# Attention reads and scores in half-size matmul tiles, with the column sums moved behind the reads

## The chip, the cores and the metric

The kernel runs on one core of a Trainium2 chip. The metric is the device time of one execution in microseconds (us). TensorE (PE in the profile, its weight loads PEld), VectorE (DVE), ScalarE (ACT), GpSimd (POOL) and the DMA queues of SyncE (SP) and GpSimd work side by side, each on its own list of instructions in order, and wait for one another by semaphores.

## The reference

Two blocks follow one another. The first is an attention in both directions between the tokens of each of 8 batches and 8 heads (512 tokens, 64 features) and 32 state rows; the second is a feed-forward with a sine-square activation.

```python
scores  = scale * x @ state.T;   a  = softmax(scores);   xread = a  @ state    # 512 x 32 for each head
scores2 = scale * state @ x.T;   a2 = softmax(scores2);  sread = a2 @ x
y = concat([xread, sread])       # tokens first, then state rows; heads side by side: 4352 x 512 in all
h = y @ w_in                     # 512 -> 2048
g = h + sin(alpha * h)**2 / (alpha + 1e-9)
out = g @ w_out                  # 2048 -> 512
```

Nothing is subtracted from the scores before the exponential in the kernel, so scores and scores2 have the same exponentials E (one is the other transposed): xread needs row sums of E, sread column sums.

## The kernel before

All the work is written as small steps of a class, and a long hand-written list, ORDER, says in which order they are issued. A step is written with its arguments, as in `sc.4.0.5`: batch 4, group 0, PSUM bank 5. Each engine runs its own instructions in the order of that list; a step waits only where it needs data or a free bank. There are eight PSUM banks, and each step that starts a new result on TensorE names its bank; it waits until the last reader of the former content is done.

For a batch b, heads come in pairs (q = 0 to 3, two heads of 64 features fill the 128 partitions) and pairs come in groups of two (g). The steps are:

- `lx` loads x, `pk` packs it by token chunk (xp), `td` transposes it by DMA on SP's queue (xT). Batch 1 has `xt` and `xc` instead (transposes on TensorE, copies on ACT and DVE).
- `sc.b.g.bank` (line 399): the scores of group g, eight matmuls. The stationary tile is xT of a pair and a chunk of 128 tokens (128 rows, 128 columns); the moving operand is stT, the transposed state of the pair with zeros outside its two blocks, so 64 columns. `ex.b.g` (line 406) takes the exponential into E on ACT.
- `rs`, `rr` (DVE) are row sums and their reciprocals, `nm` (POOL) normalises E to A, `ad` transposes A by DMA on SP's queue into AT.
- `m.b.s.banks` (line 488) multiplies the state by w_in, in tiles of 64 rows and 32 columns, and `me` (line 496) copies that to M on ACT or DVE. `h.b.f` (line 537; `hg`, line 552, in batch 0) is then M times AT, 512 columns: 128 features of h for all tokens of the batch.
- `si`, `sq`, `gt` (lines 560, 569 or 201, 576) apply the activation; gt frees h's bank. `o.b.st.f0.f1` (line 587) sums over features into the output, `oc` copies it out of PSUM, `os` stores it from SP's queue.
- `w.b.bank` (line 450): the state reads. 16 matmuls: stationary, a pair of heads of xp for a chunk of tokens (128 rows, 128 columns); moving, E of that pair, 64 columns. Half of the result mixes two heads and is not used. `cs.b` (line 461) adds the column sums to the same bank, 8 matmuls with a stationary of ones of 64 columns, even and odd heads to the two halves of the partitions. `rc` and `xs` (DVE, lines 468 and 471) divide and put the result into xs_all, from which "batch" 8 (the state rows of all batches) takes its h (line 543).

In ORDER w and cs of a batch are neighbours in some batches and apart in others; cs.0, cs.2, cs.3 and cs.6 are issued directly ahead of an m block, and cs.7 and cs.5 directly after one another. The TensorE warm-up (`warm_up`) plays a part at the start only.

Of the kernel before, what the change touches and what calls it, by code (L numbers as in the profile page):

```python
# [9 lines left out]
ACT = mybir.ActivationFunctionType  # L10
ALU = mybir.AluOpType
AX = mybir.AxisListType
BF16 = mybir.dt.bfloat16
FP32 = mybir.dt.float32
# [27 lines left out]
o.0.2.5.6 xc.1.1.1.V xc.1.0.0.A o.0.0.6.7 xc.1.0.1.V o.0.0.7.8 o.0.2.6.7 sc.1.1.5 gt.0.10 sc.1.0.4  # L42
m.0.3.6.2 ex.1.0 o.0.2.7.8 me.0.3.0.V o.0.1.0.3.3 me.0.3.1.V o.0.1.3.6 hg.0.13.0.6 o.0.1.6.7 ex.1.1
rs.1.0 hg.0.13.1 m.1.3.2.4 si.0.13 o.0.1.7.8 rr.1.0 rs.1.1 nm.1.0.0.4.G o.0.1.8.9 hg.0.12.0.5
o.0.3.8.9 rr.1.1 hg.0.12.1 me.1.3.0.V o.0.0.8.9 nm.1.1.0.4.G o.0.1.9.10 o.0.0.9.10 me.1.3.1.V
si.0.12 o.0.0.10.11 o.0.3.9.11 sq.0.13.G ad.1 hg.0.15.0.2 sq.0.12.A o.0.1.10.12 hg.0.15.1 gt.0.12
o.0.2.8.10 si.0.15 o.0.2.10.11 gt.0.13 o.0.0.11.12 hg.0.14.0.4 sq.0.15.A hg.0.14.1 o.0.3.11.13
si.0.14 gt.0.15 o.0.0.12.13 o.0.1.12.13 o.0.3.13.14 sq.0.14.A pk.2.0.V o.0.1.13.14 pk.2.1.V h.1.2.5
gt.0.14 h.1.4.6 td.2 si.1.2 lx.3.0.1 h.1.0.2 si.1.4 o.0.0.13.15 sq.1.2.V h.1.1.4 si.1.0 gt.1.2
sq.1.4.G o.0.3.14.16 si.1.1 o.0.2.11.13 sq.1.0.A oc.0.3.V h.1.6.5 sq.1.1.G gt.1.4 o.0.2.13.14 os.0.3  # L50
h.1.3.0 si.1.6 gt.1.0 o.0.1.14.16 si.1.3 sq.1.6.G h.1.13.6 gt.1.1 oc.0.1.A o.0.2.14.15 o.0.0.15.16
si.1.13 h.1.15.2 sq.1.3.G gt.1.6 os.0.1 o.0.2.15.16 oc.0.0.A h.1.5.4 sq.1.13.G oc.0.2.V si.1.15
h.1.7.3 os.0.0 gt.1.3 o.1.1.0.1.5 si.1.5 os.0.2 h.1.8.1 sq.1.15.G gt.1.13 o.1.1.1.2 si.1.7
o.1.2.0.2.7 sq.1.5.A o.1.1.2.3 sq.1.7.G h.1.12.0 gt.1.15 si.1.8 h.1.9.6 gt.1.5 o.1.2.2.3 si.1.12
sq.1.8.G o.1.2.3.5 gt.1.7 si.1.9 o.1.1.3.4 h.1.10.2 sq.1.12.A pk.3.1.V h.1.11.4 sq.1.9.G gt.1.8
o.1.2.5.6 si.1.10 o.1.2.6.7 gt.1.12 h.1.14.3 si.1.11 sq.1.10.G o.1.2.7.8 gt.1.9 sc.2.1.1 si.1.14
o.1.1.4.7 sq.1.11.A pk.3.0.V sq.1.14.G o.1.1.7.8 gt.1.10 td.3 o.1.2.8.9 sc.2.0.0 o.1.1.8.9 gt.1.11
o.1.1.9.10 ex.2.0 o.1.3.0.2.6 gt.1.14 o.1.3.2.4 o.1.2.9.10 o.1.3.4.5 o.1.2.10.12 ex.2.1 o.1.2.12.13
rs.2.0 o.1.1.10.11 m.2.2.2.4.3.0 rr.2.0 rs.2.1 o.1.2.13.14 nm.2.0.0.4.G me.2.3.0.A o.1.2.14.15 w.0.1
rr.2.1 me.2.2.1.A me.2.3.1.V o.1.3.5.6 nm.2.1.0.4.G me.2.2.0.A o.1.3.6.7 o.1.2.15.16 cs.0 oc.1.2.A  # L60
m.2.0.3.4.0.2 ad.2 rc.0 o.1.3.7.8 me.2.1.1.A o.1.3.8.9 sc.3.0.7 xs.0.1 me.2.1.0.A o.1.1.11.12 os.1.2
me.2.0.0.V sc.3.1.2 me.2.0.1.A o.1.1.12.13 o.1.3.9.10 xs.0.0 o.1.3.10.11 ex.3.0 o.1.1.13.16 ex.3.1
rs.3.0 o.1.3.11.13 oc.1.1.A o.1.3.13.14 rr.3.0 h.2.0.0 rs.3.1 nm.3.0.0.4.G os.1.1 o.1.3.14.16 si.2.0
rr.3.1 h.2.1.3 oc.1.3.V nm.3.1.0.4.G h.2.2.4 h.2.8.1 os.1.3 h.2.3.7 lx.4.0.1 ad.3 si.2.2 o.1.0.0.3.2
si.2.8 sq.2.0.V o.1.0.3.4 sq.2.2.G gt.2.0 h.2.4.5 si.2.1 o.1.0.4.6 si.2.3 sq.2.8.G o.1.0.6.7 gt.2.2
h.2.9.6 si.2.4 o.2.3.0.1.0 o.1.0.7.8 sq.2.1.G o.1.0.8.9 sq.2.3.A gt.2.8 o.1.0.9.10 h.2.5.4 si.2.9
gt.2.3 o.1.0.10.11 sq.2.4.G o.1.0.11.12 si.2.5 h.2.7.1 gt.2.1 o.1.0.12.13 sq.2.9.A sq.2.5.G
o.1.0.13.14 gt.2.4 o.1.0.14.15 si.2.7 o.1.0.15.16 o.2.0.0.1.7 gt.2.9 o.2.0.1.2 oc.1.0.A h.2.6.3
sq.2.7.G gt.2.5 o.2.3.1.2 os.1.0 o.2.3.2.3 si.2.6 h.2.10.5 pk.4.1.V pk.4.0.V o.2.3.3.4 sq.2.6.A
o.2.3.4.5 gt.2.7 h.2.11.6 td.4 si.2.10 h.2.12.2 gt.2.6 si.2.11 o.2.0.2.3 sq.2.10.G o.2.0.3.4  # L70
o.2.3.5.6 si.2.12 h.2.15.4 h.2.13.1 sq.2.11.A gt.2.10 sq.2.12.G o.2.0.4.5 si.2.15 h.2.14.3 gt.2.11
o.2.3.6.7 si.2.13 o.2.0.5.6 sq.2.15.G gt.2.12 o.2.0.6.8 si.2.14 o.2.3.7.9 sq.2.13.A o.2.3.9.10
gt.2.15 sq.2.14.G o.2.0.8.11 gt.2.13 o.2.0.11.12 sc.4.0.5 sc.4.1.6 gt.2.14 o.2.3.10.12 ex.4.0
o.2.3.12.13 w.1.2 cs.1 o.2.0.12.13 rc.1 o.2.3.13.15 ex.4.1 o.2.3.15.16 m.3.0.4.1.3.5 rs.4.0 oc.2.3.A
o.2.0.13.14 me.3.1.0.A o.2.0.14.15 os.2.3 me.3.0.0.V o.2.1.0.1.6 me.3.0.1.A o.2.1.1.2 o.2.0.15.16
rr.4.0 rs.4.1 o.2.1.2.3 me.3.1.1.A nm.4.0.0.4.G h.3.1.0 oc.2.0.A o.2.1.3.4 rr.4.1 xs.1.0
m.3.2.3.4.1.5 si.3.1 nm.4.1.0.4.G os.2.0 xs.1.1 h.3.0.7 me.3.2.0.V h.3.2.2 ad.4 me.3.3.0.V o.2.1.4.6
lx.5.0.1 o.2.2.0.1.3 me.3.3.1.V si.3.2 o.2.2.1.3 si.3.0 h.3.6.1 sq.3.1.V sq.3.2.G me.3.2.1.V
h.3.14.5 si.3.6 o.2.2.3.4 gt.3.1 o.2.2.4.5 sq.3.0.G si.3.14 o.2.2.5.7 gt.3.2 o.2.2.7.8 sq.3.6.A
o.2.2.8.9 h.3.8.4 sq.3.14.G gt.3.0 h.3.5.0 si.3.8 gt.3.6 h.3.15.2 si.3.5 o.2.2.9.10 sq.3.8.G gt.3.14  # L80
o.2.2.10.11 h.3.9.7 si.3.15 h.3.7.1 si.3.9 sq.3.5.G gt.3.8 o.2.2.11.13 si.3.7 h.3.10.5 sq.3.9.G
o.2.2.13.14 sq.3.15.A gt.3.5 o.2.2.14.15 h.3.4.4 si.3.10 gt.3.15 o.2.1.6.7 sq.3.7.G o.2.1.7.8 si.3.4
o.2.2.15.16 o.2.1.8.10 sq.3.10.A gt.3.9 o.2.1.10.11 sq.3.4.G gt.3.7 o.2.1.11.13 oc.2.2.A o.2.1.13.14
gt.3.10 o.2.1.14.16 os.2.2 h.3.3.0 gt.3.4 oc.2.1.A h.3.12.2 si.3.3 pk.5.1.V o.3.2.0.1.7 os.2.1
m.4.2.1.3.5.6 pk.5.0.V si.3.12 sq.3.3.V td.5 o.3.3.0.1.4 me.4.2.1.V me.4.2.0.A o.3.2.1.2 sq.3.12.G
o.3.3.1.2 me.4.3.0.A o.3.2.2.3 gt.3.3 o.3.3.2.3 h.3.11.1 me.4.3.1.A gt.3.12 h.4.10.3 si.3.11 h.4.9.5
si.4.10 h.4.12.0 sq.3.11.V h.4.11.6 si.4.9 gt.3.11 sq.4.10.G o.3.2.3.5 si.4.12 o.3.2.5.7 sq.4.9.A
o.3.2.7.8 gt.4.10 sq.4.12.G o.3.2.8.10 si.4.11 o.3.2.10.11 gt.4.9 o.3.3.3.5 sq.4.11.A o.3.3.5.6
gt.4.12 o.3.3.6.8 m.4.0.2.1.3.5 gt.4.11 o.3.3.8.9 me.4.1.1.V me.4.0.1.A h.3.13.0 me.4.0.0.A h.4.8.6
me.4.1.0.V h.4.15.1 si.3.13 h.4.2.5 si.4.8 sq.3.13.V h.4.1.2 lx.6.0.1 si.4.2 gt.3.13 o.3.2.11.12  # L90
o.3.1.0.2.3 si.4.15 o.3.1.2.3 sq.4.8.V o.3.1.3.4 sq.4.2.G si.4.1 gt.4.8 o.3.3.9.12 sq.4.15.A h.4.3.0
sq.4.1.G gt.4.2 o.3.3.12.13 h.4.13.6 si.4.3 gt.4.15 o.3.3.13.15 si.4.13 sq.4.3.G o.3.3.15.16 gt.4.1
h.4.6.5 oc.3.3.A o.3.2.12.13 h.4.5.1 sq.4.13.G si.4.6 gt.4.3 os.3.3 h.4.14.2 si.4.5 o.3.0.0.1.4
sq.4.6.G o.3.2.13.14 gt.4.13 si.4.14 o.3.0.1.4 sq.4.5.A h.4.4.0 sq.4.14.G gt.4.6 o.3.0.4.5 h.4.0.6
si.4.4 gt.4.5 o.3.1.4.6 si.4.0 sq.4.4.G gt.4.14 o.3.2.14.16 w.2.5 sq.4.0.A pk.6.1.V o.3.1.6.7
oc.3.2.A h.4.7.1 pk.6.0.V gt.4.4 sc.5.0.2 td.6 si.4.7 o.3.1.7.8 sc.5.1.7 gt.4.0 o.3.1.8.9 o.3.0.5.6
ex.5.0 sq.4.7.G o.3.0.6.8 o.3.1.9.11 os.3.2 o.3.0.8.9 gt.4.7 o.3.0.9.12 cs.2 ex.5.1 rs.5.0
m.5.0.0.6.1.2 o.3.0.12.13 rr.5.0 me.5.0.0.A rs.5.1 o.4.3.0.1.7 nm.5.0.0.4.G o.3.0.13.14 me.5.0.1.A
o.3.0.14.15 rr.5.1 o.3.1.11.12 me.5.1.1.V o.3.1.12.13 me.5.1.0.A nm.5.1.0.4.G o.4.3.1.3 rc.2
o.3.0.15.16 o.4.3.3.4 o.3.1.13.14 oc.3.0.A ad.5 o.3.1.14.15 xs.2.0 m.6.0.0.6.2.1 xs.2.1 o.4.3.4.5  # L100
me.6.1.1.V me.6.1.0.A sc.6.1.4 os.3.0 sc.6.0.5 me.6.0.1.A o.4.3.5.6 me.6.0.0.V o.4.3.6.7 ex.6.0
o.4.3.7.8 o.4.0.0.1.2 o.3.1.15.16 ex.6.1 rs.6.0 w.3.1 oc.3.1.A cs.3 rr.6.0 m.5.2.6.0.5.4 rs.6.1
nm.6.0.0.4.G os.3.1 o.4.3.8.9 me.5.2.0.A me.5.2.1.V o.4.0.1.2 o.4.3.9.10 me.5.3.0.A o.4.3.10.11
rr.6.1 o.4.2.0.1.3 rc.3 nm.6.1.0.4.G o.4.2.1.2 me.5.3.1.A h.5.8.6 o.4.3.11.12 xs.3.1 h.5.9.0 si.5.8
ad.6 xs.3.0 o.4.0.2.3 o.4.3.12.14 o.4.2.2.4 h.5.4.5 si.5.9 o.4.3.14.15 sq.5.8.V h.5.3.4 si.5.4
gt.5.8 o.4.2.4.5 sq.5.9.G h.5.0.1 si.5.3 o.4.3.15.16 o.4.0.3.4 si.5.0 sq.5.4.G o.4.2.5.6 oc.4.3.V
o.4.2.6.8 sq.5.3.A gt.5.9 h.5.1.6 os.4.3 sq.5.0.G h.5.5.7 gt.5.4 si.5.1 o.4.2.8.10 si.5.5 gt.5.3
h.5.2.0 sq.5.1.G o.4.2.10.11 gt.5.0 o.4.2.11.12 si.5.2 h.5.14.5 lx.7.0.1 sq.5.5.A gt.5.1 h.6.3.4
o.4.2.12.13 si.5.14 gt.5.5 o.4.2.13.14 sq.5.2.G o.4.0.4.5 o.5.0.0.1.1 si.6.3 o.4.2.14.15 h.6.6.6
sq.5.14.A sq.6.3.G gt.5.2 o.4.0.5.6 h.5.13.7 si.6.6 gt.5.14 o.4.0.6.8 si.5.13 sq.6.6.G o.4.0.8.9  # L110
gt.6.3 o.4.0.9.11 sq.5.13.A o.4.0.11.12 h.6.2.0 gt.6.6 h.5.12.5 si.6.2 gt.5.13 o.4.2.15.16 h.6.4.4
si.5.12 sq.6.2.G o.4.0.12.13 oc.4.2.V o.4.0.13.14 si.6.4 o.4.0.14.15 o.4.1.0.1.6 os.4.2 o.4.1.1.2
# [551 lines left out]
```

The softmax here doesn't subtract the row's maximum and nothing guards it: scores larger than these inputs give would overflow.

## Time and profile before

| | |
|---|---|
| device time, median of 3 runs (lowest, highest) | 221.16 us (221.13, 221.43) |
| span of the profiled execution | 221.2 us; the view of the core gives 221.2 us too, and no other time lies around it |
| TensorE clock granted | 1.000 |
| score matmuls, line 399, 128\*128 with 64 columns | 128, median 193 ns each |
| state reads, line 450, 128\*128 with 64 columns | 128, median 193 ns each |
| column sums, line 461, 128\*64 with 128 columns | 64, median 219 ns each |
| weight loads of lines 399, 450, 461 | medians 98, 98, 110 ns |
| exponentials, line 406 | 16, median 597 ns |

A matmul's row lasts from its start to the end of its way through the array; matmuls overlap, so what one takes from the engine is read from the distance between starts. A shape such as 128\*64 is the stationary tile, rows by columns; "128x64 bf16" is the moving operand. An entry "idle ... <- X" says what ended the idle time before a row.

### The profile page before, as it was taken

What the parts mean: (1) busy time and instruction counts of PE and PEld (TensorE: products, weight loads), DVE (VectorE), ACT (ScalarE), POOL (GpSimd) and SP (SyncE); (2) the same over time, 40 slices, a digit from 0 to 9 for tenths busy, and PEclk for the clock granted to TensorE, in tenths of its full rate; (3) what the DMA queues carried; (4) which work ended last, traced back from release to release, by engine and by line L of the source; (5) the groups of instructions that cost most, each with busy time, mean ns of one, the idle gap of its engine ahead of it and who ended that gap; (6) DMA issues with size and microseconds to landing.
All of it is one profiled execution on the core that took longest, in us unless ns stands there. A gap on an engine that the chain in (4) does not pass through costs nothing.

```text
span 221.2 us, 4330 instructions
## 1 busy us (share of the span) xinstructions
PE 215.7 (97%) x1619; PEld 106.0 (48%) x1619; DVE 162.4 (73%) x286; ACT 173.5 (78%) x297; POOL 107.1 (48%) x115
## 2 busy tenths in 40 slices
PE   7999999999999999999999999999999999999994
PEld 3664454444444444444454444445445555665452
DVE  3468986999678979988888778889766988571201
ACT  3589878998899979998996999798857897685111
POOL 6866626595388728934863377363501072121000
PEclk9999999999999999999999999999999999999999
DMA  6999995953549518375325437380220211012042
GB/s 172 198 206 204 205 203 87 174 199 73 119 127 158 96 50 150 44 190 61 81 41 125 126 95 94 108 117 17 47 99 0 98 47 47 0 50 95 1 142 96
DMA packets 38052, 23.48 MB, mean 106 GB/s; under 512 B 20992, under 2 KB 33680, under 8 KB 38032
## 3 DMA queue, kind: packets, MB, share of 16 engines
q0 software_dynamic: 11648, 8.13, 26.1%
q1 hardware_dynamic: 26128, 15.08, 26.1%
q8 instruction: 12, 0.20, 0.4%
q14 instruction: 8, 0.07, 0.1%
q10 hardware_dynamic: 256, 0.01, 0.1%
HBM read 17.44 MB, written 8.91 MB: 119 GB/s over the span
## 4 chain that ended last, share of the span: by engine, by line
PE 93%; ACT 3%; DMA 2%; SPq 0%; issue 0%
PE o_ps L587 54%; PE h_ps L537 22%; PE m_ps L488 4%; PE h_ps L543 3%; PE h_ps L552 3%; DMA x<-in_x_dram 2%; PE s_ps L399 2%; PE warm_ps L303 2%; PE w_ps L450 2%; PE w_ps L461 1%; PE x_ps L361 1%; ACT L226 1%; ACT s L560 1%; ACT M L496 1%; PE x_ps L376 0%; PE st_ps L333 0%
## 5 line engine op out<-in xcount | busy, mean ns | idle before, releaser
L587 PE MATMUL o_ps<-w_out_sb,gT 128*128 128x512 bf16 (+2 forms) x560 | 137.7, 373 | 0.0
L576 DVE SCALAR_TENSOR_TENSOR gT<-s,inva_sb,h_ps 128x512 bf16<-128x512 bf16 (+1 forms) x144 | 96.6, 714 | 18.8 <-POOL s L201 9.6
L201 POOL TENSOR_TENSOR s<-s 128x512 bf16<-128x512 bf16 (+1 forms) x76 | 76.7, 1021 | 65.9 <-ACT s L560 62.4
L560 ACT ACTIVATE s<-h_ps,alpha_sb 128x512 bf16<-128x512 f32 (+1 forms) x144 | 88.8, 671 | 10.5 <-PE h_ps L543 4.3
L587 PEld LDWEIGHTS <-gT 128*128 128x128 bf16 x560 | 52.3, 98 | 60.3 <-issue 5.0
L537 PE MATMUL h_ps<-AT,M 128*128 128x512 bf16 x224 | 60.8, 379 | 0.0
L537 PEld LDWEIGHTS <-M 128*128 128x128 bf16 x224 | 21.7, 98 | 25.9 <-issue 0.4
L569 ACT ACTIVATE s<-s 128x512 bf16<-128x512 bf16 (+1 forms) x53 | 31.4, 595 | 0.8
L201 POOL TENSOR_TENSOR A<-E,rR 128x512 bf16<-128x512 bf16 x16 | 16.6, 1048 | 25.7 <-ACT o_sb L595 12.7
L595 ACT COPY o_sb<-o_ps 128x512 f32<-128x512 f32 (+2 forms) x24 | 13.7, 571 | 16.6 <-PE o_ps L587 16.5
L496 ACT CAST M<-m_ps 128x512 bf16<-128x512 f32 x35 | 18.6, 594 | 8.2 <-PE m_ps L488 8.1
L496 DVE CAST M<-m_ps 128x512 bf16<-128x512 f32 x29 | 18.9, 679 | 2.5 <-PE m_ps L488 2.1
L595 DVE COPY o_sb<-o_ps 128x512 f32<-128x512 f32 x11 | 7.6, 691 | 13.0 <-PE o_ps L587 12.9
L303 PE MATMUL warm_ps<-warm 128*128 128x128 bf16 (+3 forms) x66 | 9.9, 295 | 1.4 <-DVE warm L209 1.2
L410 DVE TENSOR_REDUCE R<-E 128x16 f32<-128x512 bf16 x16 | 10.4, 658 | 1.1 <-ACT E L406 0.9
L201 DVE TENSOR_TENSOR s<-s 128x512 bf16<-128x512 bf16 (+1 forms) x15 | 6.2, 415 | 6.8 <-ACT s L560 6.7
L488 PE MATMUL m_ps<-w_in_sb,stT 64*32 64x512 bf16 x256 | 10.2, 382 | 0.0
L468 DVE RECIPROCAL rC<-w_ps 128x128 f32<-128x128 f32 x8 | 7.6, 948 | 3.2 <-PE w_ps L461 3.2
L406 ACT ACTIVATE E<-s_ps 128x512 bf16<-128x512 f32 x16 | 8.8, 601 | 1.4 <-PE s_ps L399 1.3
L552 PE MATMUL h_ps<-AT,M 128*128 128x512 bf16 x32 | 9.4, 380 | 0.4 <-ACT M L496 0.4
L543 PE MATMUL h_ps<-xs_all,w_in_sb 128*128 128x256 bf16 x64 | 9.1, 273 | 0.0
L560 ACT ACT_TABLE_LOAD x5 | 6.4, 1283 | 2.2 <-PE h_ps L537 1.1
(56 smaller groups left out, 104.3 us busy)
## 6 DMA issues: line engine op xcount, KB each, us to landing
out_dram<-o_sb SPq DMA_DIRECT2D x33, 256.0 KB, 2.3
xnat<-in_x_dram POOLq DMA_DIRECT2D x7, 512.0 KB, 7.7
w_in_sb<-in_moe_w_in_dram POOLq DMA_DIRECT2D x4, 512.0 KB, 10.3
w_out_sb<-in_moe_w_out_dram POOLq DMA_DIRECT2D x4, 512.0 KB, 16.3
x<-in_x_dram SPq DMA_DIRECT2D x4, 256.0 KB, 4.3
st_nat<-in_state_dram POOLq DMA_DIRECT2D x1, 256.0 KB, 5.7
out_dram<-o_sb SPq DMA_DIRECT2D x1, 192.0 KB, 1.9
s<-in_state_dram SPq DMA_DIRECT2D x1, 128.0 KB, 2.1
```

What stands on the lines that cost most here:

```text
L201: {"V": k.nc.vector, "G": k.nc.gpsimd}[eng].tensor_tensor(out, a, b, ALU.mult)
L303: k.nc.tensor.matmul(wp[:, :cols], k.warm[:, 0:k.P], k.warm[:, :cols], start=True, stop=True)
L488: k.nc.tensor.matmul(k.t["m", b, s + n, g][o0:o0 + k.Ns, :], k.stT[k.half(r), b * k.G + g, c0:c0 + k.Ns], k.w_in_sb[k.half(r), 2 * g + h, ...
L496: k.copy(eng)(k.t["M", b][:, g, s * k.FW:(s + 1) * k.FW], k.t["m", b, s, g][:])
L537: k.nc.tensor.matmul(hp[:, :n], k.t["M", t][:, g, fs], k.t["AT", t][:, g, :], start=(g == 0), stop=(g == k.G - 1),)
L543: k.nc.tensor.matmul(hp[:, :n], k.w_in_sb[:, q, fs], k.xs_all[:, q].rearrange("p b j -> p (b j)"), start=(q == 0), stop=(q == k.Q - 1),)
L552: k.nc.tensor.matmul(k.t["h", t, f][:], k.t["M", t][:, g, f * k.P:(f + 1) * k.P], k.t["AT", t][:, g, :], start=(g == 0), stop=(g == k.G - 1),)
L560: k.nc.scalar.activation(s[:, :n], k.t["h", t, f][:, :n], ACT.Sin, scale=k.alpha_sb[:, f:f + 1])
L569: k.nc.scalar.activation(s2[:, :n], s[:, :n], ACT.Square)
L576: k.nc.vector.scalar_tensor_tensor(gT[:, :n], k.t["s2", t, f][:, :n], k.inva_sb[:, f:f + 1], k.t["h", t, f][:, :n], ALU.mult, ALU.add,)
L587: k.nc.tensor.matmul(k.t["o", t, st, half][:, cols], k.t["gT", t, f][:, rows], k.w_out_sb[:, f, cols], start=(f == 0), stop=(f == k.FT - 1),)
L595: k.copy(eng)(o_sb[:, cols], k.t["o", t, st, half][:, cols])
```

## The change

Two functions are rewritten or new, and the order is adapted.

- In `w` each matmul is split by head: a stationary of 64 columns (one head), 32 moving columns, to the head's own half of the partitions. 32 matmuls a batch instead of 16; the unused quarter blocks are no longer computed.
- `cs` stands directly behind `w` in every batch.
- For batches 1 to 7 `sc2` takes the place of the two `sc` steps. Each matmul takes one head: 64 rows of xT and of stT, 32 moving columns; even heads (r = 0) use rows 0 to 63 and write to one bank, odd heads (r = 1) rows 64 to 127 and another bank. 32 matmuls a batch instead of 16, in the order chunk, pair, head. `ex2.b.r` takes the exponential of the heads of one bank and puts them to their old places in E. Batch 0 keeps `sc` and `ex`. The bank numbers are the ones that the two `sc` steps had, in the order in which they stood; `sc2` stands where the second of them stood.

```diff
+    def sc2(k, b, *banks):
+        for r in range(2):
+            k.t["sc", b, r] = k.ps(banks[r], [k.P, k.G, k.C, 2, k.Ns], FP32, "s_ps")
+        for i in range(k.C):
+            for q in range(k.Q):
+                for r in range(2):
+                    g, h = q // 2, q % 2
+                    c = (2 * h + r) * k.Ns
+                    k.nc.tensor.matmul(
+                        k.t["sc", b, r][:, g, i, h, :], k.t["xT", b][k.half(r), i, q, :],
+                        k.stT[k.half(r), b * k.G + g, c:c + k.Ns], start=True, stop=True,
+                    )
+    def ex2(k, b, r):
+        E = k.new(b, "E", k.epool, [k.P, k.G, k.C, k.P], BF16)
+        k.nc.scalar.activation(
+            E[:].rearrange("p g c (h r j) -> p (g c h) r j", r=2, j=k.Ns)[:, :, r, :],
+            k.t["sc", b, r][:].rearrange("p g c h j -> p (g c h) j"), ACT.Exp, scale=k.scale,
+        )
...
     def w(k, b, bank):
...
         for q in range(k.Q):
             for i in range(k.C):
-                k.nc.tensor.matmul(
-                    wc[:, q, 0:2 * k.Ns], k.pair(b, i, q),
-                    E[:, q // 2, i, (q % 2) * 2 * k.Ns:(q % 2 + 1) * 2 * k.Ns],
-                    start=(i == 0), stop=(i == k.C - 1),
-                )
+                for r in range(2):
+                    c = (q % 2 * 2 + r) * k.Ns
+                    k.nc.tensor.matmul(
+                        wc[k.half(r), q, r * k.Ns:(r + 1) * k.Ns],
+                        xp[:, i, 2 * q + r, :], E[:, q // 2, i, c:c + k.Ns],
+                        start=(i == 0), stop=(i == k.C - 1),
+                    )
```

In ORDER, with the neighbours on TensorE (the rest of the list is as it was; ex becomes ex2 in place):

```diff
-o.0.2.6.7 sc.1.1.5 gt.0.10 sc.1.0.4 m.0.3.6.2
+o.0.2.6.7 gt.0.10 sc2.1.5.4 m.0.3.6.2
-sc.2.1.1 ... o.1.2.8.9 sc.2.0.0 o.1.1.8.9
+o.1.2.8.9 sc2.2.1.0 o.1.1.8.9
-w.0.1 ... o.1.2.15.16 cs.0 oc.1.2.A m.2.0.3.4.0.2 ... o.1.3.8.9 sc.3.0.7 ... o.1.1.11.12 ... sc.3.1.2 ... o.1.1.12.13
+w.0.1 cs.0 ... o.1.2.15.16 oc.1.2.A m.2.0.3.4.0.2 ... o.1.3.8.9 ... o.1.1.11.12 ... sc2.3.7.2 ... o.1.1.12.13
-o.2.0.11.12 sc.4.0.5 sc.4.1.6 gt.2.14 o.2.3.10.12
+o.2.0.11.12 sc2.4.5.6 gt.2.14 o.2.3.10.12
-w.2.5 ... sc.5.0.2 ... o.3.1.7.8 sc.5.1.7 ... o.3.1.8.9 ... cs.2 ex.5.1 rs.5.0 m.5.0.0.6.1.2
+w.2.5 cs.2 ... o.3.1.7.8 sc2.5.2.7 ... o.3.1.8.9 ... ex2.5.1 rs.5.0 m.5.0.0.6.1.2
-sc.6.1.4 os.3.0 sc.6.0.5 ... w.3.1 oc.3.1.A cs.3 rr.6.0 m.5.2.6.0.5.4
+os.3.0 sc2.6.4.5 ... w.3.1 cs.3 oc.3.1.A rr.6.0 m.5.2.6.0.5.4
-w.4.2 ... o.5.2.4.5 sc.7.1.5 gt.6.1 sc.7.0.0 o.5.2.5.7 ... h.6.13.6 rs.7.0 cs.4
+w.4.2 cs.4 ... o.5.2.4.5 gt.6.1 sc2.7.5.0 o.5.2.5.7 ... h.6.13.6 rs.7.0
-w.5.1 ... o.5.3.13.14 ... w.7.4 gt.7.7 si.7.0 cs.7 os.5.3 cs.5 h.7.5.3
+w.5.1 cs.5 ... o.5.3.13.14 ... w.7.4 cs.7 gt.7.7 si.7.0 os.5.3 h.7.5.3
```

w.1 with cs.1, and w.6 with cs.6, stood together already.

## The prediction

> **What bounds the kernel now.** I read the page's head first, then its chain, then TensorE's rows by shape, and last the timelines around the steps that change.
>
> ```profile
> span 221.2 us, 4330 instructions
> ...
> PE 215.7 (97%) x1619; PEld 106.0 (48%) x1619; DVE 162.4 (73%) x286; ACT 173.5 (78%) x297; POOL 107.1 (48%) x115
> ...
> PEclk9999999999999999999999999999999999999999
> ...
> PE 93%; ACT 3%; DMA 2%; SPq 0%; issue 0%
> ```
>
> TensorE is busy for 97% of the span and carries 93% of the chain. From 28 to 205 us the busy time by windows is 177.00 of 177.00 us, at a granted clock of 1.00. So from there on a nanosecond added to TensorE's stream is a nanosecond of span, and one taken out is won, as long as nobody else becomes late. The profiled span, 221.2 us, is as good as the median of the three runs (221.16), so I add the sum to 221.2 without a correction. A measurement of this kernel can tell about 0.2%, 0.44 us, from no change: under 220.7 is faster, over 221.6 slower.
>
> TensorE's timeline around the reads of batch 0 (start, length, line, shape, count) gives all prices:
>
> ```profile
> 55.82 0.60 PE L587 MATMUL o_ps<-w_out_sb,gT 128*128 128x512 bf16 x2
> 56.26 0.63 PE L450 MATMUL w_ps<-E,xp 128*128 128x64 bf16 x16
> 56.72 0.81 PE L587 MATMUL o_ps<-w_out_sb,gT 128*128 128x512 bf16 x3
> 57.47 0.41 PE L461 MATMUL w_ps<-E,ones 128*64 128x128 bf16 x8
> 57.81 0.63 PE L488 MATMUL m_ps<-w_in_sb,stT 64*32 64x512 bf16 x16
> 58.37 0.39 PE L587 MATMUL o_ps<-w_out_sb,gT 128*128 128x512 bf16 x1
> ```
>
> Lengths overlap, so I subtract starts.
> - *Same shape.* 56.72 - 56.26 = 0.46 us for 16 state reads is 29 ns each; the two o matmuls before took 216 and 216 (+10 once, below). The single rows give 55.5 ns at 128 columns, 109 at 256, 162.5 at 384, 216 at 512: columns / 2.4 plus 2.4 ns, with the next load hidden.
> - *A change of tile shape.* Three o matmuls should take 0.65 us, but 57.47 - 56.72 is 0.75. In the single rows each of the 46 changes after 12 us between 128\*128, 128\*64 and 64\*32 adds 92 to 108 ns, mostly 93 to 96: I take 94. The first load in the new shape is exposed on top: 10 ns for 128\*128 or 64\*32, 24 for 128\*64 (first matmuls of 390, 387 and 243 ns against 379, 376 and 219). So 104 ns, or 118 into 128\*64.
> - *Column halves run side by side.* The eight column-sum matmuls start in pairs 4 ns apart, a pair each 55 ns; both of the first pair are late by the same 24 ns, so the two loads ran together.
>
> **Reads and column sums (w, cs).** Each batch's 16 reads of 128\*128 with 64 columns become 32 of 128\*64 with 32 columns: 16 pairs. A pair's stream is 32 / 2.4 + 2.4 = 15.7 ns, but its loads need 24, and steady rows start a load 1 to 2 ns after the previous matmul: I take 27 ns. The row of today's pair (29) and a load just hidden (26) are near; an unhidden load is 24 + 15.7 = 40, loads one after the other 54. Gain: 8 x 16 x (29 - 27) = 0.26 us. What it costs is the shape. Today w needs no change of shape and cs has both. With cs behind w the pair shares them, but cs loses its old neighbours: cs.0 and cs.2 stood ahead of an m block (57.47 to 57.81 above), so one exit served as m's entry: one more change each. cs.7 and cs.5 ran as one block of 16:
>
> ```profile
> 171.56 0.63 PE L450 MATMUL w_ps<-E,xp 128*128 128x64 bf16 x16
> 172.12 0.64 PE L461 MATMUL w_ps<-E,ones 128*64 128x128 bf16 x16
> 172.69 0.60 PE L537 MATMUL h_ps<-AT,M 128*128 128x512 bf16 x2
> ```
>
> They are split: two more. Batches 1, 3, 4 and 6 stay equal (there w is only drawn into the shape). Four changes, one of them into 128\*64: 118 + 3 x 104 = 0.43 us. Net **+0.17 us** (from -0.2 at 24 ns a pair to +1.8 at 40). cs needs only E, long ready; rc and xs keep their order on DVE, and rc may start earlier, which costs nothing.
>
> **Scores (sc2).** Batches 1 to 7 change 16 matmuls of 128\*128 with 64 columns (464 ns) into 32 of 64\*128 with 32, even heads on rows 0 to 63, odd heads on 64 to 127, one bank each. No row of before has the shape 64\*128; the m block (64\*32), where row halves start 3 to 4 ns apart, is nearest. A pair's step lies between 15.7 ns (the stream, by the line through all columns seen) and 29 (the row of 64 columns, the shortest step that the trace has). I take 22, the middle, and keep both ends. Loads of 128 columns were exposed by 10 ns only, so a step of 15.7 would hide them.
>
> Each sc2 stands between 128\*128 matmuls, so it enters and leaves: 2 x 104 = 208 ns, against 16 x (29 - 22) = 112 saved: +96 ns for each of batches 2 to 7, **+0.58 us** (0.0 at 15.7 ns, +1.25 at 29). The trace cannot show that 64\*128 is a change. The Trainium skill (TensorEngine Tiling (Array Packing), Tiling Modes, Key Properties) says that changing the mode, not just the tile, drains TensorE, and lists 64x128 as a mode of its own; that would make it 208 ns, against 0 if only column tiles cost.
>
> The same page (Performance Considerations, Instruction Overhead) speaks against the change: about 60 cycles for each matmul, so that one with a single column takes as long as one with 60, and no tiling factor should be taken from a dimension that is already small. Today's 64 columns at 29 ns agree; an estimate by that page, 60 / 2.4 = 25 ns a pair, would make the scores dearer by 7 x 16 x 3 = 0.34 us than my 22.
>
> Batch 1 is different, because its xT is made by copies just ahead:
>
> ```profile
> 28.97 0.91 DVE L385 COPY xT<-x_ps 128x512 bf16<-128x512 bf16 x2 [0.62 <-ACT xT L385]
> ...
> 29.50 0.73 PE L399 MATMUL s_ps<-stT,xT 128*128 128x64 bf16 x16
> 30.16 0.41 PE L488 MATMUL m_ps<-w_in_sb,stT 64*32 64x512 bf16 x8
> ```
>
> The second copy (heads 2 and 3) ends at 29.88 and releases TensorE at 29.94. Today heads 4 to 7 go first (sc.1.1), then 0 and 1, and only the last four matmuls wait, 94 ns. sc2 goes through all heads for each chunk, so its third matmul already needs that copy: TensorE stands from 29.5 to 29.94, with the entry inside that wait. Then 16 x 22 = 0.35 and the change to m, 0.09: 0.88 us in place of 0.66, **+0.22 us** (+0.12 to +0.33). Batch 3 likewise: sc.3.1 had 0.17 us between the copy that frees its bank (me.2.1.1.A) and its start, and the 0.23 us of sc.3.0 ahead of it go: **+0.06 us**. The other sc2 blocks have 0.1 us or more; sc.4 starts 0.1 us after its transposed xT lands (issue at 72.55 plus the median 4.3 us), all of it in one DMA as before. No DMA is moved: steps of TensorE alone change place.
>
> **The new wait.** ex2.b.0 fills only even heads, so rs.b.0 needs both exps. On ACT they stand back to back:
>
> ```profile
> 53.62 1.09 ACT L406 ACTIVATE E<-s_ps 128x512 bf16<-128x512 f32 x2
> ...
> 54.25 0.69 DVE L410 TENSOR_REDUCE R<-E 128x16 f32<-128x512 bf16 x1
> ```
>
> So rs.2.0 moves from 54.25 to about 54.73, 0.48 us. In batches 3, 5, 6 and 7 it is 0.45 to 0.5 too; rs.1.0 and rs.4.0 start after the second exp already. Behind it on DVE queue rr, rs.b.1 and a copy of M or o_sb; behind those POOL's nm and SP's transpose ad, with the output stores behind it. The cover: A^T of batch 2 lands at 57.45 + 3.0 = 60.45 and h.2 starts at 61.44; for batch 5 123.0 and 125.48, the others have 7 us and more, save batch 1, whose rs does not move. DVE itself waits 1.25 us after batch 2's block and 0.94 after batch 3's. I price it at **0.1 us** (0 to 0.5: the wait uncovered once). The exps keep their size; their write goes in runs of 32, and ACT's 591 to 628 ns stay within the same cover.
>
> **Sum:** 0.17 + 0.58 + 0.22 + 0.06 + 0.1 = +1.13 us, so 221.2 + 1.1 = **222.3 us**.
>
> **Rivals.**
> - *Faster (10%): a change to 64\*128 is free.* Place: the two ends of each sc2. With 15.7 ns a pair batches 2 to 7 win 6 x 16 x 13.3 = 1.28 us; batch 1 still loses 0.12, batch 3 0.06, w 0.17: 220.3 us. It decides below about 40 ns a change (12 changes, 1.28 - 0.35 - 0.44 left). For it: no row of that shape. Against it: all shapes that the trace has pay 92 or more, and 64\*32 has row halves too.
> - *No change (13%): changes cost, halves stream.* At 15.7 ns a pair batches 2 to 7 come out even, batch 1 +0.12, w between -0.2 and +0.17: 221.2 to 221.6.
> - *Much slower (13%): halves do not overlap.* Reads at 40 ns a pair: 8 x 16 x 13 = 1.7 more, 224.0; at 54 it is 225.8. Scores one after the other, 31 ns a pair: +1.1, 223.4. Against it: the column-sum pairs and the m block run side by side.
> - *My forecast (64%)*, 221.7 to 223.5: the upper end has 29 ns a score pair (+0.78) and 30 ns a read pair (+0.38).
>
> The range is 221.0 to 224.5: it begins where the second rival does, less the spread of the runs, and leaves out the free change and the worst of the third rival. Faster 0.10, same 0.13, slower 0.77.
>
> **What would show it.** Right: from an o row to the first 64\*128 row about 0.31 us, and the same out again; 64\*128 and 128\*64 pairs at 15 to 29 ns; TensorE's wait at 29.5 to 29.94; rs.2.0 right behind the second exp; TensorE without other gaps. Wrong: o rows 216 ns ahead of sc2 (the free change), pairs of 40 ns or more, or an h matmul of batch 2 or 3 that waits for A^T or M.

## The result and the profile after

| | before | after |
|---|---|---|
| device time, median (lowest, highest) | 221.21 us (221.13, 221.43; 6 runs) | 224.09 us (223.12, 225.86; 6 runs) |
| ratio after / before, 95% interval | | 1.0125 (1.0091 to 1.0160) |
| span of the profile shown | 221.2 us | 224.0 us |
| TensorE clock granted | 1.000 | 1.000 |

The change costs 2.9 us. The forecast was 222.3 us, 1.1 us more than before, in a range of 221.0 to 224.5: the sign and the range hold, the size does not, and the narrower 221.7 to 223.5, which had 64% of the chances, does not hold the median either. In the runs from here on the device time lies about 1.9 us above the span; a span of 221.2 us would be 223.1 us, which no run of before has. So the profile of before that the prediction used (span 221.2 us) is of an execution that began slowly: against a second profile of before (span 219.2 us, 221.06 us) it loses 2 us between 6 and 10 us, and all its later rows stand 1.9 to 2.1 us later. Up to 10.3 us its matmuls of 128 columns start 107 ns apart, those of the second profile 55 ns from 5.3 us on; the granted clock reads 1.000 in both. I compare with the second one.

The page of after, its head, chain and DMA queues:

```profile
span 224.0 us, 4804 instructions
...
PE 215.4 (96%) x1859; PEld 103.5 (46%) x1859; DVE 162.7 (73%) x286; ACT 173.6 (78%) x297; POOL 107.0 (48%) x115
...
PEclk9999999999999999999999999999999999999999
...
q8 instruction: 14, 0.23, 0.4%
...
PE 82%; DMA 8%; ACT 4%; DVE 2%; POOL 2%; issue 1%; SPq 0%; POOLq 0%; ACTq 0%
```

Two things differ from the page of before. TensorE's part of the chain fell from 93% to 82% and DMA's rose from 2% to 8%. That alone proves no new wait, as the second profile of before has 86% and 6%; the waits are read below. And the program has 474 instructions more (4804 against 4330). The program is itself read over the DMA engines, in packets of 16 KB of queue q8, one for about 120 pairs of weight load and matmul on TensorE: 14 packets instead of 12. TensorE's own new work is read from its timeline (start, length, line, shape, count), at the reads of batch 0 and the scores of batch 3:

```profile
55.98 0.60 PE L609 MATMUL o_ps<-w_out_sb,gT 128*128 128x512 bf16 x2
56.51 0.68 PE L472 MATMUL w_ps<-E,xp 128*64 128x32 bf16 x32
57.04 0.39 PE L483 MATMUL w_ps<-E,ones 128*64 128x128 bf16 x8
57.37 0.82 PE L609 MATMUL o_ps<-w_out_sb,gT 128*128 128x512 bf16 x3
58.12 0.62 PE L510 MATMUL m_ps<-w_in_sb,stT 64*32 64x512 bf16 x16
58.67 0.82 PE L609 MATMUL o_ps<-w_out_sb,gT 128*128 128x512 bf16 x3
59.43 0.57 PE L412 MATMUL s_ps<-stT,xT 64*128 64x32 bf16 x32
59.93 2.12 PE L609 MATMUL o_ps<-w_out_sb,gT 128*128 128x512 bf16 x9
```

By starts: three o matmuls of 216 ns and the entry into 64\*128 take 59.43 - 58.67 = 0.76 us, so the entry is about 0.10; the single rows give 96 ns, and 13 for the first loads, by which the second pair starts late. The 32 half-height score matmuls and the way out take 59.93 - 59.43 = 0.50 us; the single rows give 89 ns and 11 for the load on the way out, and 25.2 ns a pair (21 and 4). The 32 reads take 57.04 - 56.51 = 0.53 us, where the 16 of before took 0.46: 31.6 ns a pair (28 and 3), and 21 for the first loads.

What TensorE waits for between 33 and 79 us, in the view of the waits (us in total, times, longest), first in after, then in the second profile of before:

```profile
PE h_ps L559 <- DMA AT<-A: 1.5, 1, 1.5
PE h_ps L559 <- DVE gT L598: 0.9, 1, 0.9
```

```profile
PE o_ps L587 <- issue: 0.2, 1, 0.2
```

TensorE's timeline of after shows the first of them; the second profile of before, shown behind it, has the same 6 o matmuls followed by h at once:

```profile
35.97 1.46 PE L609 MATMUL o_ps<-w_out_sb,gT 128*128 128x512 bf16 x6
38.97 0.81 PE L559 MATMUL h_ps<-AT,M 128*128 128x512 bf16 x3 [1.54 <-DMA AT<-A]
```

```profile
35.60 1.46 PE L587 MATMUL o_ps<-w_out_sb,gT 128*128 128x512 bf16 x6
36.89 0.81 PE L537 MATMUL h_ps<-AT,M 128*128 128x512 bf16 x3
```

Step by step against the second profile of before, after ends 4.84 us later: 0.12 from the start, 1.9 of TensorE's own work, 1.71 for the transposed A of batch 1, 1.05 ahead of h.2.13 for gt.2.7, and 0.1 ahead of the scores of batch 4. "Own work" means here and below what TensorE's changed steps take longer, without waits. This profile is the slowest run of after; the median is 1.8 us shorter, and the fastest of the six, 223.12 us, is before plus the 1.9 us of own work.

### The profile page after: what moved, and what is told of

Read it like the earlier page. It is cut to its first block, busy times and chain, and to the rows that moved or that the text cites. A ratio compares the mean times of both kernels' runs of the same rounds, so it can differ in the third digit from the quotient of the medians.

```text
span 224.0 us, 4804 instructions
## 1 busy us (share of the span) xinstructions
PE 215.4 (96%) x1859; PEld 103.5 (46%) x1859; DVE 162.7 (73%) x286; ACT 173.6 (78%) x297; POOL 107.0 (48%) x115
## 4 chain that ended last, share of the span: by engine, by line
PE 82%; DMA 8%; ACT 4%; DVE 2%; POOL 2%; issue 1%; SPq 0%; POOLq 0%; ACTq 0%
PE o_ps L609 47%; PE h_ps L559 19%; DMA xnat<-in_x_dram 4%; PE m_ps L510 3%; PE h_ps L565 3%; DMA AT<-A 2%; PE w_ps L472 2%; PE h_ps L574 2%; DMA x<-in_x_dram 2%; POOL A L200 2%; PE s_ps L412 2%; PE warm_ps L302 1%; ACT s L582 1%; PE w_ps L483 1%; DVE xp L347 1%
## 5 line engine op out<-in xcount | busy, mean ns | idle before, releaser
L302 PE MATMUL warm_ps<-warm 128*128 128x128 bf16 (+3 forms) x66 | 8.6, 271 | 1.4 <-DVE warm L208 1.2
L419 ACT ACTIVATE E<-s_ps 128x512 bf16<-128x512 f32 x14 | 7.7, 603 | 0.4 <-PE s_ps L412 0.4
```

The costliest lines, as they stand in the source:

```text
L302: k.nc.tensor.matmul(wp[:, :cols], k.warm[:, 0:k.P], k.warm[:, :cols], start=True, stop=True)
```

## The experiments

The kernels are before or after with small edits. The expectations of the first four do not have the instruction fetch yet. In them one reading is that TensorE's own work and two waits, both caused by the new order, make up the whole; the other is that the wait for batch 1 is due to the faster start of the profiled execution. The later ones set "theory F" (the waits come from where a 16 KB instruction fetch falls) against these. Each time is compared with runs of before that were taken with it: medians 221.31 us for experiments 1 to 4 and 221.51 for 5 to 8. Experiments 1, 9 and 10 are single runs; 9 and 10 have one run of before beside them, 220.83 us.

**1. Before once more**, unchanged, for a profile with a normal start.

> The kernel before, unchanged, for a second profile. Theory A (the sum): the whole difference of 2.9 us is made after the 28th microsecond, by TensorE's own time (17 shape changes at 104 to 118 ns, read pairs at 31.6 ns, score pairs at 25.2 ns, as the profile after has them) and one late chain (1.06 us); the start is noise that a wait of TensorE for the transposed A of batch 1 swallows, so this profile may start up to 1.9 us sooner than the first one and still end within 0.3 us of it. Theory B (the start): the first profile happened to have a slow start of 1.9 us, and with a fast one TensorE has no wait for that transpose; then the span here is about 219.3 us, and the wait of 1.7 us at h.1.2 in the profile after belongs to the change.

Measured: 221.06 us, span 219.2. It starts about as early as after does, and does not wait for the transposed A of batch 1. So an early start alone does not make the wait.

**2. The reads alone**: the new `w` with `cs` behind it; scores as before.

```diff
+                for r in range(2):
+                        wc[k.half(r), q, r * k.Ns:(r + 1) * k.Ns],
+                        xp[:, i, 2 * q + r, :], E[:, q // 2, i, c:c + k.Ns],
...
-w.2.5 ... cs.2 ex.5.1
+w.2.5 cs.2 ... ex.5.1
```

> Only the reads in half-width matmuls with the column sums behind; scores as before. Theory A: four more shape changes, 0.43 us, and 8 x 16 pairs at 31.6 ns where 29 stood, 0.33 us: about 222.0 us (+0.76), and no new wait. Theory C (waits are all): TensorE's extra time is swallowed by waits elsewhere, 221.2 us.

Measured: 223.71 us, ratio 1.0121 (1.0104 to 1.0139), span 221.8. TensorE's own steps are 0.76 us longer: 8 x 16 x (31.6 - 29) = 0.33 for the pairs and 0.43 for four shape changes. Of the span's 2.65 us over experiment 1 another 0.45 stands at the start, and the rest, 1.45 by the starts, is one wait ahead of the scores of batch 4, in a place that the edit does not touch. Neither reading had it (222.0 and 221.2 us):

```profile
73.14 2.54 PE L589 MATMUL o_ps<-w_out_sb,gT 128*128 128x512 bf16 x11
76.99 0.64 PE L399 MATMUL s_ps<-stT,xT 128*128 128x64 bf16 x16 [1.31 <-DMA xT<-xp]
```

Of the transpose td.4 that it waits for, 15 of 16 landings come between 75.23 and 75.38 us, the 16th at 76.94. A 16 KB packet of the instruction queue began at 74.92 us and took 938 ns, to 75.86; the last packet of the transpose ends at 75.88. The trace does not name a packet's DMA engine; that the late landing is of the engine which carried the instructions is inferred from this. In the second profile of before that fetch comes at 76.5 us, after td.4 has landed (74.77 to 74.90).

**3. The scores alone**: `sc2` and `ex2` for batches 1 to 7; reads and column sums as before.

```diff
-sc.2.1.1 ... sc.2.0.0
+sc2.2.1.0
```

> Only the scores head by head; reads and column sums as before. Theory A: 13 shape changes at 104 ns, 1.35 us, less 7 x 16 x (29 - 25) ns, 0.45 us, plus some 0.3 us of wait in batch 1, plus the late chain through POOL (row sums after both exps, then the normalisation, then the load of batch 4's x, then its packing on DVE, then gt.2.7, then h.2.13), 1.06 us: about 223.4 us (+2.2). Theory C: without the late chain 222.4 us.

Measured: 223.34 us, ratio 1.0096 (1.0079 to 1.0113), span 221.9. Own work about +1.2 us, and a wait of 1.42 us for the transposed A of batch 1. There is no wait of more than 0.1 us ahead of h.2.13, for which I had put 1.06: the number expected (223.4) came out for another reason. Here the third instruction fetch comes at 34.1 us, in the middle of the transposes that SP issues from 33.27 us on; in before at 39.3 us.

**4. After with the load of x for batch 4 ahead of `nm.3.0`** on POOL, to take away the wait ahead of h.2.13, which came through this load.

```diff
-rs.3.1 nm.3.0.0.4.G ... h.2.3.7 lx.4.0.1 ad.3
+rs.3.1 lx.4.0.1 nm.3.0.0.4.G ... h.2.3.7 ad.3
```

> The changed kernel with the load of batch 4's x (lx.4.0.1) issued on POOL ahead of batch 3's normalisation (nm.3.0) in place of behind it. Theory A: the load starts at least 2 us sooner, DVE's packing no longer waits for it, gt.2.7 is on time, and TensorE's wait of 1.06 us ahead of h.2.13 goes: 223.0 us in place of 224.1. Rival: another wait stands behind it (the slow packing copy of 1.28 us beside POOL's work) and at most 0.3 us come back: 223.8 us.

Measured: 228.91 us, ratio 1.0344 (1.0314 to 1.0373): far off both numbers. POOL issued the load at 56.85 us, and it ran beside the transposes ad.2. The DMA issues from 57 to 66 us (queue, KB, median us to landing), here and then in after:

```profile
xnat<-in_x_dram POOLq DMA_DIRECT2D x1, 512.0 KB, 9.1
out_dram<-o_sb SPq DMA_DIRECT2D x2, 256.0 KB, 7.3
AT<-A SPq DMA_TRANSPOSE x1, 8.2
```

```profile
out_dram<-o_sb SPq DMA_DIRECT2D x3, 256.0 KB, 2.9
xnat<-in_x_dram POOLq DMA_DIRECT2D x1, 512.0 KB, 8.2
AT<-A SPq DMA_TRANSPOSE x2, 3.0
```

The transpose took 8.2 us in place of 3.0, and h.2.0 waited for it. The place of the load behind `nm` had kept the two apart; nothing is won there.

**5. Before with 32 more instructions at the start**: eight early warm-up groups of two matmuls of 128 columns become four of 32. All else is before, unchanged.

```diff
-warm_up.2.128.3 ex.0.0 warm_up.2.128.4 lx.1.0.1
+warm_up.4.32.3 ex.0.0 warm_up.4.32.4 lx.1.0.1
```

> The kernel before, with eight of the early warm-up groups (two matmuls of 128 columns) cut into four matmuls of 32: 16 more matmuls and 16 more weight loads on TensorE ahead of the first scores, nothing else. Theory F (instruction fetch): the 16 KB fetches of the program are tied to the number of instructions issued, so those after the early stage come some 0.5 to 5 us sooner; if one falls into the transposes of ad.1 (33 to 37 us) or td.4 (74 to 77 us), h.1 or sc.4 waits 1.4 to 1.6 us more, as in the two halves: 222.5 to 224.2. Rival (the waits come from the changed order and form of the scores and reads): 16 more instructions in a stage in which TensorE waits anyway cost nothing, 221.2 to 221.5.

Measured: median 223.62 us, ratio 1.0082 (1.0050 to 1.0114), span 222.2. Both waits appear, in the view of the waits from 33 to 79 us:

```profile
PE s_ps L399 <- DMA xT<-xp: 1.7, 1, 1.7
PE h_ps L537 <- DMA AT<-A: 0.8, 1, 0.8
```

By the starts they are 1.85 and 1.04 us, almost all of the 3.0 us of span. The fetches moved from 39.3 to 33.8 us and from 76.5 to 75.9, into ad.1 and into td.4, which is later here. The theory's numbers (222.5 to 224.2) hold, the rival's (221.2 to 221.5) do not: nothing of before but the warm-up was changed. The six runs reach from 221.96 to 226.97 us, so the waits are not the same in every execution.

**6. The reads alone with 16 matmuls and 16 loads fewer at the start**: sixteen warm-up groups of two matmuls of 128 columns become one of 256.

```diff
-warm_up.2.128.3 ex.0.0 warm_up.2.128.4
+warm_up.1.256.3 ex.0.0 warm_up.1.256.4
```

> The reads-only kernel (223.7), with sixteen early warm-up groups of two matmuls of 128 columns made one of 256: 16 matmuls and loads fewer ahead of everything, the same columns. Theory F: the fetch that fell into td.4's transposes at 74.9 us is put off by some us and misses them: the wait of 1.56 us ahead of sc.4 goes and 222.1 is left (before plus the reads' own 0.76). If the fetch hits another transpose instead, up to 223.7. Rival (the wait belongs to the reads' new form): unchanged, 223.6 to 223.9.

Measured: 222.09 us, ratio 1.0022 (1.0009 to 1.0036), span 219.7. The wait ahead of the scores of batch 4 is gone: the fetch falls at 75.7 us, 5.5 us behind SP's issue of td.4 (70.20), where it fell 4.0 us behind it in experiment 2 (74.92 and 70.97), and the two no longer meet. From 74 to 79 us the DMA view has not one transpose packet left beside it.

```profile
DMA packets 1, 0.02 MB, mean 3 GB/s; under 512 B 0, under 2 KB 0, under 8 KB 0
q8 instruction: 1, 0.02, 1.4%
```

What is left of experiment 2 is the reads' own 0.5 to 0.8 us.

**7. After with the same 16 matmuls and loads fewer.**

> The kernel after, with the same 16 early warm-up matmuls and loads fewer. Theory F: the fetch at 34.1 us moves later and misses ad.1's transposes: the wait of 1.4 to 1.7 us at h.1 goes, and 222.6 to 223.3 is left (before, plus own work of 1.95, less or plus a wait that another fetch makes). Rival: unchanged, 224.1.

Measured: 223.24 us, ratio 1.0078 (1.0055 to 1.0101), that is 1.7 us (1.2 to 2.2) over before. The third fetch comes at 40.6 us and h.1 does not wait. The DMA view from 33 to 39.2 us, in after and then here:

```profile
q8 instruction: 1, 0.02, 1.0%
...
AT<-A SPq DMA_TRANSPOSE x1, 5.6
```

```profile
q0 software_dynamic: 1042, 0.53, 67.2%
q1 hardware_dynamic: 1056, 0.26, 22.9%
q14 instruction: 1, 0.01, 0.3%
...
AT<-A SPq DMA_TRANSPOSE x1, 3.2
```

Without the q8 packet the transpose lands after 3.2 us, as in before (3.2); with it after 5.6. The q14 packet, 8 KB and 0.3 us, comes ahead of ad.1 in every profile. All twelve profiles divide in this way. In six a q8 packet begins between 33.3 and 34.1 us, and ad.1 lands 4.6 to 5.6 us after its issue: the two of after, and experiments 3, 4, 5 and 9. In the other six it begins at 39.3 us or later, and ad.1 lands after 3.1 to 3.2 us. Kernels with the old scores and kernels with the new ones stand on both sides (experiment 5 among the late, 7 among the others), so the place of the packet decides, not the form of the scores.

**8. Only `cs` moved behind `w`** in before: the same instructions in another order.

```diff
-w.2.5 ... cs.2 ex.5.1
+w.2.5 cs.2 ... ex.5.1
```

> The kernel before with only the column sums cs moved straight behind their reads w; the reads stay full matmuls, the instructions on TensorE are as many as before. Both theories: four more changes of shape at 94 to 104 ns, +0.4 us, 221.6 to 221.8, and the fetches where they were (39.3 and 76.5 us). If the move of cs does more than that (a later wait for the sums), over 222.0.

Measured: 221.77 us, ratio 1.0008 (0.9992 to 1.0024). The measurement cannot tell this from no change, but the trace can: the profiled run (222.81 us) has a wait of 1.35 us near 28 us, of which 0.6 is for x and 0.5 for its transposed copies, ahead of everything that was moved, and 0.40 us more at the end, which is four added shape changes of 94 ns and a load of 24. The fetches come at 40.6 and 77.3 us, behind the transposes.

**9. After with 64 moving columns in the reads**, where it has 32; the neighbouring head runs along.

```diff
-wc[k.half(r), q, r * k.Ns:(r + 1) * k.Ns], ... E[:, q // 2, i, c:c + k.Ns],
+wc[k.half(r), q, 0:2 * k.Ns], ... E[:, q // 2, i, c - r * k.Ns:c + (2 - r) * k.Ns],
```

> The kernel after with 64 moving columns in place of 32 in every half-width read of batches 1 to 7 (the neighbouring head's columns run along, so each head's read holds that head and its neighbour, and the sums behind it are not those of the reference). Theory: the read pair's 31.6 ns is set by its two loads of 128 rows x 64 columns, so up to that time columns are free: 64 columns take 25 to 27 ns by the 21 ns of 32 and the pace stays 31 to 33 ns a pair, the whole time is that of after, 223 to 225 us. Rival: the columns that stream set the pace, and 32 more of them add 13 ns to each of the 128 pairs: 45 ns a pair, 1.7 us longer.

Measured: 224.11 us in one run, where after in experiment 10 has 223.36; 0.4 us of the difference lies at the start. The edit holds for all eight batches, and the added half of the result is not used. The 128 pairs take as long as in after (3.99 us for the 248 steps within the blocks, in both). So it is not the columns that set the 31.6 ns. That leaves the two loads of 128\*64 that each pair needs, or a fixed cost of an instruction in this shape; the runs do not part these.

**10. After once more**, unchanged.

> The kernel after, unchanged, for a second profile. Theory F: the fetch falls at the same instruction, near 34 us, and the wait at h.1 comes again with 1.0 to 1.7 us; the wait of 1.06 us for gt.2.7, behind a copy of x that took 1.28 us where 0.42 is usual, hangs on a chance meeting of two engines and is gone or under 0.3 us: 223.0 to 223.5. Rival: both waits belong to the change and come again, 224.0 to 225.8.

Measured: 223.36 us, span 221.5. The wait for the transposed A of batch 1 comes again, with 0.67 us by the starts, less than expected, as the fetch came at 33.3 us, near the start of the transposes. The wait ahead of h.2.13 does not come again. The copies of x for batch 4 on DVE, in the first profile of after and then in this one:

```profile
72.70 1.62 DVE L347 COPY xp<-xnat 128x1024 bf16<-128x1024 bf16 x2 [1.11 <-DMA xnat<-in_x_dram]
```

```profile
70.96 0.76 DVE L347 COPY xp<-xnat 128x1024 bf16<-128x1024 bf16 x2 [0.72 <-DMA xnat<-in_x_dram]
```

Experiments 7 and 9 do not have the long copy either. What lengthened it in that one execution stays open.

No version came out below before: each part of the change has a price of its own on TensorE, with or without the waits.

## Why the prediction was right and where it was not

| term | predicted, us | measured, us |
|---|---|---|
| read pairs, 8 x 16 | -0.26 (27 ns) | +0.33 (31.6 ns) |
| four more shape changes at w and cs | +0.43 | +0.43, alone +0.40 |
| scores of batches 2 to 7 | +0.58 (22 ns a pair) | +0.88 (25.2 ns a pair) |
| scores of batch 1 | +0.22 | +0.25 to +0.35 |
| scores of batch 3, its bank | +0.06 | about +0.03 |
| later `rs` | +0.1 | none for A^T of batches 2 to 7 |
| wait at h.1 for the transposed A of batch 1 | not in the sum | +0.7 to +1.7, none in experiment 7 |
| wait ahead of h.2.13 | not in the sum | +1.05 in one profile, 0.15 at most in three others |
| sum | +1.1 | +1.85 to +1.95 own work, +2.9 with the waits (medians) |

- *Shape changes: right.* 64\*128 is a shape of its own: 96 ns in and 89 out, where 94 was taken from the other shapes. This is what decided the sign; the rival with a free change would have shown o rows 216 ns ahead of `sc2` in place of 312.
- *Halves side by side: right.* The two matmuls of a pair start 3 to 4 ns apart in the reads and in most score blocks, and mostly 5 to 8 in two. Behind the first pair of a block, which takes the first loads, no pair takes 40 ns, the expected wait in batch 1 apart.
- *The pair's step: mis-sized twice.* I took the middle between 15.7 and 29 ns for scores, and 27 for reads from a load that is just hidden. Measured were 25.2 and 31.6. With these two values my own sum gives 0.17 + 0.59 = 0.76 for the reads and 0.58 + 0.31 = 0.89 for batches 2 to 7: all of the difference between 1.1 and 1.9. Why a read pair takes 31.6 ns stays open (experiment 9).
- The Trainium skill (TensorEngine Tiling (Array Packing), Performance Considerations, Instruction Overhead) gives about 60 cycles a matmul, 25 ns as an estimate; the 25.2 ns of the score pairs, whose two matmuls run side by side, agree, and the 31.6 ns of the read pairs lie above it. I had weighed this rule and put the middle in its place.
- *The new wait on both exponentials: right in mechanism, and covered.* DVE's idle time ahead of `rs` grew as expected, in the groups of the second profile of before and of after:

```profile
L410 DVE TENSOR_REDUCE R<-E 128x16 f32<-128x512 bf16 x16 | 10.4, 658 | 1.2 <-ACT E L406 0.9
```

```profile
L430 DVE TENSOR_REDUCE R<-E 128x16 f32<-128x512 bf16 x16 | 10.4, 658 | 4.1 <-ACT E L419 4.1
```

- No h of batches 2 to 7 waits for its transposed A in any profile of after. The list of what stands behind `rs` left out POOL's load of x, but its delay (issued at 64.50 us in after, 63.23 in experiment 7, 61.66 in the second profile of before) made TensorE wait in one profile only.
- *What was missing: the program itself.* The sum priced the 240 added matmuls and their loads by TensorE's time alone. Their instructions also have to be fetched, over the same DMA engines, and the fetches then fall elsewhere. The sentence "No DMA is moved" was wrong: the fetch at 39.3 us moved to 34.1 and met ad.1. Experiment 5 shows it without any of the change, 7 takes the wait out of after.
- *The noise was set too low.* The prediction wanted to tell 0.44 us from no change. Runs of before in the experiments reach from 220.79 to 222.12 us, those of after from 223.12 to 225.86.

So that the range held was in part luck: it reached to 224.5 for another reason, halves that do not overlap, and the wait that filled it was on no list.

## What to carry to other kernels

Cutting matmuls that are already short into halves that run side by side gains little: with 32 columns the pair took 25 to 32 ns where one full matmul of 64 columns took 29, and each entry into a new tile shape and each exit cost some 90 to 100 ns. In a kernel bound by one engine, count the instructions that a change adds: they move the instruction fetches, and a fetch that falls into a DMA transpose with no slack behind it can cost more than the instructions do (2.9 us of waits for 32 instructions in experiment 5). Before a small difference is put down to a change, shift the fetches with a few instructions in an idle stage and see whether it stays.

## What the runs showed of the hardware

- One 16 KB instruction packet (0.9 to 1.9 us in the profiles of before and after) put off the landing of a transpose: of ad.1 from 3.1 to 3.2 us after its issue to between 4.6 and 5.6, of td.4 from 4.3 to 5.9 and 6.0 (experiments 5 and 2). td.3, with slack behind it, went from 4.3 to between 5.9 and 6.0 in five profiles, and nothing waited for it. How the delay arises stays open: of td.4 one landing of 16 was late, of ad.1 all, and in experiment 10 the packet had ended (34.27 us) when the first packet of ad.1 began (34.31).
- The third fetch comes with the 344th to 358th weight load of TensorE in every profile, whether 16 early ones are added or taken away. In time that moved it by 5.5 us (39.3 to 33.8) in before and by 6.5 us (34.1 to 40.6) in after, and by 1.7 us in the reads-only kernel.
- With a plain load of 512 KB beside it a transpose took 8.2 us in place of 3.0 (experiment 4). In the second profile of before ad.4, issued at 81.55 us, stands beside such a load, issued at 81.47, and takes 6.8 us.
- 32 and 64 moving columns take the same time in 128\*64 pairs, 31.6 ns (experiment 9).
